# Spectral filter and sine MLP on one core: first MLP chunk of 384 tokens, sign of the imaginary filter set in the head's copy, batch 0's last stage in groups of five

## The chip, the core and the metric

The kernel runs on one core of a Trainium2 chip. The metric is the device time of one execution in microseconds (us). Three runs of the kernel before took 786.11, 786.23 and 787.95 us; the median is 786.23 us.

The engines are named as in the profile: PE is the matrix engine (PEld its weight loads), DVE the vector engine, ACT the scalar engine, POOL the GpSimd engine, and SP the engine that issues most DMAs. PSUM is the memory that PE writes to and DVE and ACT read from; SBUF is the main on-chip memory.

## The reference

```python
X = np.fft.rfft(x, axis=1)                      # x: 8 batches x 3008 positions x 256 channels
y = np.fft.irfft(X * (filt_r + 1j * filt_i), n=3008, axis=1)
x = y.reshape(8 * 3008, 256)
h = x @ w_in                                    # 256 -> 2048
g = h + np.sin(alpha * h) ** 2 / (alpha + 1e-9)
out = g @ w_out                                 # 2048 -> 256
```

Each batch goes through a Fourier filter along its 3008 positions, and each position (a token) then goes through an MLP with 2048 hidden units.

## The kernel before

**The spectral part.** 3008 is 94 times 32, so a transform of a batch is done in four matrix stages, which the profile shows by the names of their PSUM tiles: `pa` (first, line 181, 16 matmuls a batch), `pb` (forward, line 201, 12 pairs), a product with the filter on DVE (lines 215, 221 and 222), `pc` (inverse, line 232, 12 pairs) and `pd` (last, line 254, 16 groups of 4). Between the stages the data go through DRAM (`d1`, `d2`) to change their layout. The last stage writes `y`, which holds two batches side by side as columns: 94 columns for each of 32 positions `n2` of one batch. The complex product needs the real and imaginary halves of `xf` swapped; two DMAs on SP do that (`xs`, lines 208 and 209), and `cross` (lines 221 and 222) multiplies the swapped half with `f_t[1]` and adds. For that, the first 64 rows of `f_t[1]` must hold the negated imaginary filter.

**Batch 0** is done in the head, before the MLP can start, with other code: lines 396 to 507. There the imaginary part is taken by a second table `e1_0`, made by `inverse_table` (lines 364 to 372: PE transposes, then one ACT copy per group, times the per-row scale `sign`, 0.125 in the upper 64 rows and -0.125 in the lower). `other_half` copies the filter to the other 64 rows on DVE. After `turn_back`, two DVE transposes, `last_0(n0, n)` makes `y` for `n` positions `n2` from `n0` on: twice `n` matmuls (line 343) and two copies from PSUM (`evac`), the first on ACT, the second on DVE.

**The MLP** runs over chunks of tokens, 12 for each pair of batches: 11 of 512 and one of 384, the sixth. For each of the 16 hidden blocks `jb` of a chunk, `hidden` does two matmuls into PSUM (`ph`, line 541), a sine on ACT (`cos_all`, line 545, four buffers) and a DVE operation (line 546) that reads both and writes `v`. `project` multiplies a token block of 128 by `w2` in two halves of 8 matmuls (`po`, line 558); ACT copies it (line 566), and SP stores it.

**Order.** The program is written out by hand, with no scheduler: every engine takes its instructions in program order. The main loop (line 648) has 8 steps for each chunk. In a step, chunk `k` gets two hidden blocks, and the chunk before gets its share of the half projections (8 for 512 tokens, 6 for 384). Chunk 0 has no projections beside it (steps 0 to 7). All spectral work of later batches is put at a step number with `put(at, fn, ...)`, and `slot` runs what is due, twice in a step. `last_0(..., spread=True)` lays its matmuls one by one between those of the MLP (`one_between`).

**Buffers.** `fps` (2 PSUM buffers) serves `pa`, `pb`, `pc` and `pd`, `hps` (4) serves `ph`, `ops` (2) serves `po`. `vp` has two buffers. They are taken in turn by `t1_0`, `t2_0`, `w_out32` (line 473, the 32-bit output weights), and then by `v` of chunk 0, 1, 2 and so on (line 538). So `v` of chunk 1 takes the buffer of `w_out32`, and its first write waits for the last reader of that.

**Weights.** POOL scales them: `weights_in` (line 482, six pieces of `w_in` times alpha) and `weights_out` (line 514, three pieces of `w_out32`; ACT does four single blocks at steps 5 to 6.5, line 512). The four loads of `x` for batch 1 (line 141) stand between these on POOL's queue, and the first of them waits for the first half of `w_out32` to land.

**The negation.** The lower copy of the imaginary filter is made unsigned in the head, since batch 0 takes its sign from `e1_0`. Two DVE operations (`negate`, line 603) put at steps 13 and 14 negate it in place for the later batches.

`evac` without an engine named goes to ACT twice and to DVE once, in turn; every call moves the turn on.

Of the kernel before, what the change touches and what calls it, by code (L numbers as in the profile page):

```python
# [10 lines left out]
FP32 = mybir.dt.float32  # L11
# [3 lines left out]
ALU = mybir.AluOpType  # L15
# [3 lines left out]
B, S, C = 8, 3008, 256  # L19
# [43 lines left out]
def kernel(  # L63
# [10 lines left out]
    nc = tc.nc  # L74
# [17 lines left out]
    def pool(name, bufs, space=None):  # L92
        kw = {} if space is None else {"space": space}
        return ctx.enter_context(tc.tile_pool(name=name, bufs=bufs, **kw))

    cpool = pool("consts", 1)
# [10 lines left out]
    hps = pool("hps", 4, PSUM)  # L107
# [7 lines left out]
    def by_half(t):  # L115

        return t.rearrange("p a (b c) -> p (a b) c", c=128)
# [16 lines left out]
    f_t = [filt_t[:, k] for k in range(2)]  # L134
# [22 lines left out]
    def evac(dst, src, on_act=None):  # L157
        flip[0] = (flip[0] + 1) % 3
        if flip[0] if on_act is None else on_act:
            marks["act"] = nc.scalar.copy(out=dst, in_=src)  # L160
        else:
            marks["dve"] = nc.vector.tensor_copy(out=dst, in_=src)  # L162
# [108 lines left out]
    e1_0 = by_half(t4_h[1])  # L271
# [24 lines left out]
    for g in range(2):  # L296
        gs = slice(12 * g, 12 * g + 12)
        for k, filt in enumerate((filt_r, filt_i)):
            for q in range(2):
                if (g, k, q) == (0, 1, 1):  # L300
# [3 lines left out]
                    out=f_t[k][64 * k + 32 * q:64 * k + 32 * q + 32, gs, :],  # L304
# [28 lines left out]
    def last_0(n0, n, own=fps, tag="f", spread=False):  # L333

        for cb in range(2):
            made = []

            def one(i, cb=cb, made=made):

                if i == 0:  # L340
                    ps = own.tile([128, 512], FP32, name=f"pd_0_{n0}_{cb}", tag=tag)
                    made.append(ps[:, 0:n * NR].rearrange("p (a r) -> p a r", r=NR))
                nc.tensor.matmul(out=made[0][:, i, :], lhsT=t4_cols[:, n0 + i, :, cb], rhs=wi0_t,  # L343
                                 start=True, stop=True)
                if i == n - 1:
                    evac(y[:, cb, 0, n0:n0 + n, :], made[0], cb == 0)

            for i in range(n):
                if spread:
                    between.append(lambda i=i, one=one: one(i))  # L350
                else:
                    one(i)
# [4 lines left out]
        nc.tensor.transpose(out=ps[:, 0:16], in_=rec, identity=id32)  # L357
        nc.vector.tensor_scalar(out=rec_t, in0=ps[:, 0:16], scalar1=-0.5, scalar2=None, op0=ALU.mult)

    sign = cpool.tile([128, 1], FP32)  # L360
    nc.vector.memset(sign[0:64], 0.125)
    nc.vector.memset(sign[64:128], -0.125)

    def inverse_table(g):

        gs = slice(8 * g, 8 * g + 8)
        ps = ops.tile([128, 8, 128], FP16, name=f"pse_{g}", tag="o")
        for i in range(8):
            for a in range(2):
                nc.tensor.transpose(out=ps[64 * a:64 * a + 64, i, :],  # L370
                                    in_=d_t[:, 8 * g + i, 64 - 64 * a:128 - 64 * a], identity=id16)
        nc.scalar.mul(e1_0[:, gs, :], ps, sign)

    warmed = []

    def warm_pe(n):

        warmed.append(n)
        ps = hps.tile([128, 512], FP32, name=f"warm_{len(warmed)}", tag="h")
        for i in range(n):  # L380
            nc.tensor.matmul(out=ps, lhsT=idle[:, 0:128], rhs=idle[:, 0:512], start=True, stop=True)  # L381

    def other_half(g, k, on_act):

        gs = slice(12 * g, 12 * g + 12)
        evac(f_t[k][64 - 64 * k:128 - 64 * k, gs, :], f_t[k][64 * k:64 * k + 64, gs, :], on_act)

    warm_pe(10)
    def cast_x0(h):
# [6 lines left out]
    for i in range(16):  # L396
        own, tag = (fps, "f") if i % 3 == 2 else (hps, "h")
        ps = own.tile([128, 512], FP32, name=f"pa_0_{i}", tag=tag)
# [21 lines left out]
    for i in range(4):  # L420
        turn(t2_0[i // 2][:, :, 32 * (i % 2):32 * (i % 2) + 32], t1_0[:, :, 32 * i:32 * i + 32])
        if i > 1:
            other_half(0, i - 2, False)
# [56 lines left out]
    def weights_in(g):  # L480
# [4 lines left out]
        if g == 0:  # L485
            after(ins, marks["products"])

    [inverse_table(g) for g in range(2)]
    for i in range(6):
        forward_0(i)  # L490
        if i % 3 == 2:
            if i == 2: inverse_table(2)
            warm_pe((4, 0)[i // 3])
    for i in range(13):
        for e in {5: [(1,0,False)],6: [(1,1,False)]}.get(i, ()):
            other_half(*e)
        if i < 12:
            product_0(i)
        if i == 11:
            reciprocals()  # L500
        if i > 0:
            inverse_0(i - 1)
        if i + 6 < 12:
            forward_0(i + 6)
        if i == 12:
            turn_back(0)
# [12 lines left out]
    for step in ([(weights_in, g) for g in range(3)] + [(s1.load_x, 0), (weights_in, 3), (s1.load_x, 1),  # L519
# [1 line left out]
                 + [(weights_out, jb) for jb in (0, 4, 8)]):  # L521
        step[0](*step[1:])
    warm_pe(12)
    last_0(0, 4)
    last_0(4, 2, hps, "h")
    warm_pe(2)

    chunks = [(pb, c0, 384 if c0 == 2560 else 512) for pb in range(B // 2)
              for c0 in [*range(0, 2561, 512), *range(2944, 2 * S, 512)]]

    v = {}
    pso = {}
# [61 lines left out]
    def put(at, fn, *args, pe=False):  # L594
        pending.append((at, len(pending), pe, fn, args))
# [1 line left out]
    for jb in range(12, 16):  # L597
        put(5 + 0.5 * (jb - 12), weights_out, jb, 1)

    def negate(i):  # L600

        gs = slice(12 * i, 12 * i + 12)
        nc.vector.tensor_scalar(out=f_t[1][0:64, gs, :], in0=f_t[1][0:64, gs, :],
                                scalar1=-1.0, scalar2=None, op0=ALU.mult)

    for i in range(2):
        put(13 + i, negate, i)
    for n0, n, at in ((6, 5, 1.5), (11, 4, 12.5), (15, 4, 14), (19, 4, 15.5), (23, 4, 17), (27, 5, 19)):
        put(at, last_0, n0, n, fps, "f", True)
    for b in range(1, B):  # L610
        s = s1 if b == 1 else Spectral(b)
        z = 48 * b
        if b > 1:
            for ch in range(4):
                put((22,27,32,37)[ch] if b == 2 else z - 92 + 7 * ch, s.load_x, ch)
        for i in range(16):
            put(6.9 + 0.35 * i if b == 1 else 36 + 0.66 * i if b == 2 else z - 67 + 0.66 * i, s.first, i, pe=True)
        for g in range(4):
            put(12.5 if b == 1 else max(z - 56, 46.5), s.load_t2, g)
        for u in range(12):  # L620
            inv = 23.5 + 1.25 * u if b == 1 else 59 + 2.1 * u if b == 2 else z - 40.8 + 2.3 * u
            fwd = inv - (6 if b == 1 else 6)
            put(fwd, s.forward, u, pe=True)
            put(fwd + (0.5 if b == 1 else 1.5), s.product, u)
            if s.fused:
                put(fwd + (4 if b == 1 else 4.5), s.cross, u)
            put(inv, s.inverse, u, pe=True)
        for ch in range(4):
            put(z - (9.5 if b == 1 and ch < 3 else (10.5, 10.5, 10.5, 3)[ch]), s.load_t4, ch)
        for u in range(16):  # L630
            put(z + (u - (5 if b == 1 else 6.5) if u < 4 else 2 * u - 9), s.last, u, pe=True)
# [59 lines left out]
```

## Time and profile before

| what | value |
|---|---|
| median of three runs | 786.23 us (786.11 to 787.95) |
| the profiled execution | 785.94 us |
| its span, first to last instruction | 784.2 us |
| PE busy | 772.0 us (98%), 5799 matmuls |
| DVE, ACT, POOL busy | 656.1 us (84%), 617.8 us (79%), 80.0 us (10%) |
| first matmul of chunk 0 (line 541) | 36.23 us |
| first matmul of chunks 1, 2, 3, 4, 5, 6 | 46.28, 65.18, 83.04, 99.77, 117.51, 133.49 us |
| granted PE clock | 1.0 throughout |

The trace holds one execution. A time such as 46.28 counts from the start of its span. A wait is put down to the engine and line that released it last. Matmuls are pipelined: one is shown as busy until its result stands, though the next starts earlier, so the work of PE is better read from the distance between two starts than from its busy share. On DVE and ACT, too, the next instruction starts up to 0.1 us before the end of the last.

### The profile page before, as it was taken

Reading aid. Unit: us, or ns where it says so; the run is one execution under the profiler, and the core shown is the slowest. Engines: PE = TensorE matmul, PEld = TensorE weight load, DVE = VectorE, ACT = ScalarE, POOL = GpSimd, SP = SyncE. Lnnn points to the kernel's source line nnn. Section 1 sums busy time; section 2 is a strip of 40 time slices with the busy share of each in tenths; the row PEclk is TensorE's granted clock in tenths of the full one; section 3 lists DMA queues with packets and bytes.
Section 4 is the critical chain, followed back from the end, with each engine's and each line's share of the span. In section 5 each row is a group of like instructions: output and inputs, shape, how many; then the busy total and the mean of one; then the engine's idle time right before and its main releaser. Section 6 shows DMA issues by size and latency. Waiting matters only on the chain.

```text
span 784.2 us, 16619 instructions
## 1 busy us (share of the span) xinstructions
PE 772.0 (98%) x5799; PEld 535.1 (68%) x5799; DVE 656.1 (84%) x1169; ACT 617.8 (79%) x1211; POOL 80.0 (10%) x125
## 2 busy tenths in 40 slices
PE   8999999999999999999999999999999999999998
PEld 4757766676667766777667766767667776766666
DVE  7897987899878997799877998799977999777773
ACT  5897988888878887888877887788887887777674
POOL 6342000300020000200020000200002000000000
PEclk9999999999999999999999999999999999999999
DMA  9956667655664546654575454845566243421111
GB/s 218 276 118 159 130 133 221 152 124 121 172 165 89 132 101 190 148 122 107 132 206 111 104 112 132 224 90 117 121 163 174 64 99 81 116 62 28 41 41 54
DMA packets 87692, 100.99 MB, mean 129 GB/s; under 512 B 14488, under 2 KB 75944, under 8 KB 87608
## 3 DMA queue, kind: packets, MB, share of 16 engines
q1 hardware_dynamic: 78032, 73.73, 34.6%
q0 software_dynamic: 9360, 26.15, 17.9%
q8 instruction: 45, 0.74, 0.4%
q14 instruction: 39, 0.32, 0.1%
q10 hardware_dynamic: 216, 0.05, 0.0%
HBM read 55.72 MB, written 46.66 MB: 131 GB/s over the span
## 4 chain that ended last, share of the span: by engine, by line
PE 90%; DMA 4%; DVE 3%; ACT 1%; SPq 1%; issue 1%; POOL 0%; DVEq 0%; ACTq 0%; POOLq 0%
PE po L558 40%; PE ph L541 39%; PE pa L181 3%; PE pd L254 2%; PE pb L201 2%; PE pc L232 2%; DVE v L546 2%; DMA d_t<-d_tbl 1%; DMA filt_t<-in_filt_i_dram 1%; SPq L586 1%; ACT cos_all L545 1%; DMA t_a<-d 0%; PE warm L381 0%; PE pc L453 0%; DMA out_dram<-o 0%
## 5 line engine op out<-in xcount | busy, mean ns | idle before, releaser
L546 DVE SCALAR_TENSOR_TENSOR v<-cos_all,ph 128x512 f16<-128x512 f32 (+1 forms) x768 | 483.2, 672 | 106.4 <-ACT cos_all L545 102.7
L545 ACT ACTIVATE cos_all<-ph 128x512 f32<-128x512 f32 (+1 forms) x768 | 411.1, 591 | 94.4 <-PE ph L541 93.5
L558 PE MATMUL po<-w,v 128*128 128x256 f16 x3008 | 389.5, 273 | 0.0
L541 PE MATMUL ph<-y,w 128*128 128x512 f16 (+1 forms) x1536 | 387.9, 375 | 1.6 <-DVE y L162 0.9
L558 PEld LDWEIGHTS <-v 128*128 128x128 f16 x3008 | 288.2, 98 | 78.4 <-issue 2.1
L541 PEld LDWEIGHTS <-w 128*128 128x128 f16 x1536 | 147.8, 98 | 103.9 <-issue 3.1
L566 ACT COPY o<-po 128x512 f32<-128x512 f32 (+1 forms) x97 | 55.7, 574 | 19.9 <-PE po L558 12.9
L204 ACT CAST xf<-pb 128x512 f16<-128x512 f32 x84 | 50.0, 595 | 13.1 <-PE pb L201 12.3
L193 POOL DMA_DIRECT2D t<-d x56 | 36.4, 670 | 203.2 <-DMA out_dram<-o 121.6
L160 ACT CAST t_h<-pa 96x512 f16<-96x512 f32 x74 | 43.3, 585 | 8.8 <-PE pa L181 8.5
L141 POOL DMA_DIRECT2D x<-in_x_dram x32 | 17.2, 537 | 297.5 <-PE pc L232 160.4
L160 ACT CAST y<-pd 128x376 f16<-128x376 f32 (+1 forms) x82 | 39.4, 480 | 8.8 <-PE pd L254 5.3
L254 PEld LDWEIGHTS <-t_a 96*128 96x128 f16 x448 | 31.3, 97 | 19.0 <-DMA t_a<-d 0.6
L160 ACT CAST g<-pc 128x512 f16<-128x512 f32 x61 | 36.2, 593 | 9.6 <-PE pc L232 9.2
L181 PE MATMUL pa<-x,wf_t 94*96 94x512 f16 x112 | 42.4, 381 | 0.6 <-ACT t_h L160 0.4
L222 DVE TENSOR_TENSOR p<-p,xs 128x512 f16<-128x512 f16 x84 | 35.7, 425 | 2.9
L254 PE MATMUL pd<-wi_t,t_a 96*128 96x94 f16 x448 | 37.2, 204 | 0.3 <-DMA t_a<-d 0.3
L221 DVE TENSOR_TENSOR xs<-xs,filt_t 128x512 f16<-128x512 f16 x84 | 35.2, 419 | 1.5 <-DMA xs<-xf 1.5
L215 DVE TENSOR_TENSOR p<-xf,filt_t 128x512 f16<-128x512 f16 x84 | 35.2, 419 | 0.0
L232 PE MATMUL pc<-p,e_t 128*128 128x256 f16 x168 | 32.1, 273 | 1.3 <-DVE t_h L162 1.3
L201 PE MATMUL pb<-t,d_t 128*128 128x256 f16 x168 | 32.1, 273 | 0.2
L162 DVE CAST y<-pd 128x376 f16<-128x376 f32 (+2 forms) x46 | 24.9, 543 | 1.8 <-PE pd L343 1.0
(66 smaller groups left out, 264.0 us busy)
## 6 DMA issues: line engine op xcount, KB each, us to landing
x<-in_x_dram POOLq DMA_DIRECT2D x30, 376.0 KB, 5.0
d<-t_h SPq DMA_DIRECT2D x28, 384.0 KB
t<-d POOLq DMA_DIRECT2D x56, 192.0 KB, 5.0
xs<-xf SPq DMA_DIRECT2D x168, 64.0 KB
d<-g SPq DMA_DIRECT2D x56, 192.0 KB
t_a<-d SPq DMA_DIRECT2D x28, 384.0 KB
out_dram<-o SPq DMA_DIRECT2D x104, 80.0 KB
w_out<-in_moe_w_out_dram SPq DMA_DIRECT2D x2, 1024.0 KB
```

The source lines that it names most:

```text
L160: marks["act"] = nc.scalar.copy(out=dst, in_=src)
L181: marks["pe"] = nc.tensor.matmul(out=ps[0:NK, :], lhsT=wf_t, rhs=self.x[ch][:, 2 * j:2 * j + 2, :], start=True, stop=True)
L193: nc.gpsimd.dma_start(out=self.t2[g][64 * p:64 * p + 64, :, :], in_=self.d1[a0:a0 + 6, :, :].rearrange("s n c -> n s c"))
L201: nc.tensor.matmul(out=ps[:, i, :], lhsT=d_t[:, s, :], rhs=self.t2[s // 6][:, s % 6, :], start=True, stop=True)
L204: nc.scalar.copy(out=self.xf[u], in_=ps)
L232: nc.tensor.matmul(out=ps[:, i, :], lhsT=e_t[:, 2 * w + i, :], rhs=pt[:, i, :], start=(k == 0), stop=(k == len(pr) - 1))
L254: nc.tensor.matmul(out=psv[:, i, :], rhs=wi_t, start=True, stop=True, lhsT=t4_h[ch // 2][0:NK, n0 % 16 + i, cb * 128:cb * 128 + 128])
L541: nc.tensor.matmul(out=ps[:, 0:n], lhsT=w1[:, cb, jb * 128:jb * 128 + 128], rhs=y_cols[:, cb, c0:c0 + n], start=(cb == 0), stop=(cb == 1))
L545: nc.scalar.activation(out=cs[:, 0:n], in_=ps[:, 0:n], func=AFT.Sin, bias=float(np.pi / 2))
L546: marks["snake"] = nc.vector.scalar_tensor_tensor(out=v[k][:, jb, 0:n], in0=cs[:, 0:n], scalar=-1.0, in1=ps[:, 0:n], op0=ALU.add, op1=ALU. ...
L558: nc.tensor.matmul(out=pso[k][:, t % 2, :], lhsT=v[k][:, jb, 128 * t:128 * t + 128], rhs=w2[:, jb, :], start=(jb == 0), stop=(jb == 15))
L566: nc.scalar.copy(out=o[:, i0:t % 2 + 1, :], in_=pso[k][:, i0:t % 2 + 1, :])
```

## The change

Three things are changed. First, the chunk of 384 tokens in the first pair of batches is the first and not the sixth; the other three pairs keep theirs. Chunk 0 then needs 5 positions `n2` (470 columns) instead of 6 before it can start, and the head makes these in one group of 5; the later groups become (5, 5), (10, 5), and then (15, 4) and on as before. Second, `other_half` for the imaginary filter multiplies by -1 while it copies. The sign of `e1_0` is then the same in all rows, so `sign` with its two memsets goes and the ACT copy takes the constant -0.125; the two `negate` operations go. Third, for batch 1 the first stage, and the forward and inverse stages, are put at other steps.

```diff
-    sign = cpool.tile([128, 1], FP32)
-    nc.vector.memset(sign[0:64], 0.125)
-    nc.vector.memset(sign[64:128], -0.125)
...
-        nc.scalar.mul(e1_0[:, gs, :], ps, sign)
+        nc.scalar.mul(e1_0[:, gs, :], ps, -0.125)
...
-        evac(f_t[k][64 - 64 * k:128 - 64 * k, gs, :], f_t[k][64 * k:64 * k + 64, gs, :], on_act)
+        if k == 0:
+            evac(f_t[0][64:128, gs, :], f_t[0][0:64, gs, :], on_act)
+        else:
+            nc.vector.tensor_scalar(out=f_t[1][0:64, gs, :], in0=f_t[1][64:128, gs, :],
+                                    scalar1=-1.0, scalar2=None, op0=ALU.mult)
...
-    last_0(0, 4)
-    last_0(4, 2, hps, "h")
+    last_0(0, 5)
     warm_pe(2)
 
-    chunks = [(pb, c0, 384 if c0 == 2560 else 512) for pb in range(B // 2)
-              for c0 in [*range(0, 2561, 512), *range(2944, 2 * S, 512)]]
+    chunks = [(pb, c0, 384 if c0 == 0 else 512) for pb in range(B // 2)
+              for c0 in [0, *range(384, 2 * S, 512)]]
+    chunks[12:] = [(pb, c0, 384 if c0 == 2560 else 512) for pb in range(1, B // 2)
+                   for c0 in [*range(0, 2561, 512), *range(2944, 2 * S, 512)]]
...
-    def negate(i):
-
-        gs = slice(12 * i, 12 * i + 12)
-        nc.vector.tensor_scalar(out=f_t[1][0:64, gs, :], in0=f_t[1][0:64, gs, :],
-                                scalar1=-1.0, scalar2=None, op0=ALU.mult)
-
-    for i in range(2):
-        put(13 + i, negate, i)
-    for n0, n, at in ((6, 5, 1.5), (11, 4, 12.5), (15, 4, 14), (19, 4, 15.5), (23, 4, 17), (27, 5, 19)):
+    for n0, n, at in ((5, 5, 1.5), (10, 5, 12.5), (15, 4, 14), (19, 4, 15.5), (23, 4, 17), (27, 5, 19)):
         put(at, last_0, n0, n, fps, "f", True)
...
-            put(6.9 + 0.35 * i if b == 1 else 36 + 0.66 * i if b == 2 else z - 67 + 0.66 * i, s.first, i, pe=True)
+            put(7.7 + 0.31 * i if b == 1 else 36 + 0.66 * i if b == 2 else z - 67 + 0.66 * i, s.first, i, pe=True)
...
-            inv = 23.5 + 1.25 * u if b == 1 else 59 + 2.1 * u if b == 2 else z - 40.8 + 2.3 * u
+            inv = 24.2 + 1.23 * u if b == 1 else 59 + 2.1 * u if b == 2 else z - 40.8 + 2.3 * u
```

The forward stage of a unit stays 6 steps ahead of its inverse stage, and `cross` 4 steps after the forward stage, so both move with `inv`.

## The prediction

> **What bounds the kernel now.** First the page: busy shares and clock.
>
> ```profile
> PE 772.0 (98%) x5799; PEld 535.1 (68%) x5799; DVE 656.1 (84%) x1169; ACT 617.8 (79%) x1211; POOL 80.0 (10%) x125
> ...
> PEclk9999999999999999999999999999999999999999
> ```
>
> PE is the bound and its clock is whole. The change leaves the number and kinds of matmuls as they are, so only the start of chunk 0 and PE's waits can move the end. I read the waits from the distance between matmul starts: undisturbed, a `ph` matmul takes 0.216 us at 512 tokens and 0.162 at 384, a `po` 0.109, a `pa` 0.22, a `pd` 0.04. What exceeds that from 36.2 us on is 11.0 us: 2.3 in chunk 0 (36.2 to 46), 0.7 to 58, 1.6 to 66, 0.6 to 76, 0.1 to 110, 1.4 at 112.9, 0.8 from 120 to 140, and 3.4 spread over the other 640 us. So anything to be won lies before 130 us. Next, who ended PE's waits there (waits of PE, 36 to 200 us: total, times, longest):
>
> ```profile
> PE pc L232 <- DVE t_h L162: 1.3, 1, 1.3
> PE ph L541 <- DVE y L162: 0.9, 1, 0.9
> PE ph L541 <- DVE v L546: 0.6, 1, 0.6
> ...
> PE pd L254 <- DMA t_a<-d: 0.3, 1, 0.3
> ```
>
> These few waits are what the change can touch. Then DVE in time order, 36 to 50 us (start, length, operation):
>
> ```profile
> 37.55 4.87 DVE L546 SCALAR_TENSOR_TENSOR v<-cos_all,ph 128x512 f16<-128x512 f32 x8 [1.10 <-ACT cos_all L545]
> 42.34 0.64 DVE L162 CAST y<-pd 128x470 f16<-128x470 f32 x1
> 42.89 3.67 DVE L546 SCALAR_TENSOR_TENSOR v<-cos_all,ph 128x512 f16<-128x512 f32 x6
> 46.78 1.29 DVE L546 SCALAR_TENSOR_TENSOR v<-cos_all,ph 128x512 f16<-128x512 f32 x2 [0.22 <-ACT cos_all L545]
> 47.98 0.68 DVE L162 CAST t_h<-pa 96x512 f16<-96x512 f32 x1
> 48.90 1.28 DVE L546 SCALAR_TENSOR_TENSOR v<-cos_all,ph 128x512 f16<-128x512 f32 x2 [0.24 <-POOL w L514]
> ```
>
> Chunk 0 is bound by DVE, 0.60 us a block; PE would need 0.43. The last row carries the forecast: the first `v` of chunk 1 starts 0.03 us after POOL's last `w2` piece. It takes the buffer of `w_out32`. POOL's own rows:
>
> ```profile
> 36.19 0.58 POOL L141 DMA_DIRECT2D x<-in_x_dram  x1 [1.48 <-PE pd L343]
> ...
> 43.27 5.59 POOL L514 TENSOR_TENSOR w<-w_out,rec_t 128x1024 f16<-128x1024 f32 x3
> ```
>
> From 36.19 to 48.87 POOL has no gap, and nothing in that queue is changed. DVE in 60 to 68 us:
>
> ```profile
> 60.82 0.95 DVE L603 TENSOR_SCALAR filt_t<-filt_t 64x3072 f16<-64x3072 f16 x1
> ...
> 63.38 0.95 DVE L603 TENSOR_SCALAR filt_t<-filt_t 64x3072 f16<-64x3072 f16 x1
> 64.25 0.54 DVE L162 CAST y<-pd 128x376 f16<-128x376 f32 x1
> ```
>
> The second negation stands ahead of the `y` copies, the last of which (65.90 to 66.44) releases chunk 2's second matmul at 66.49.
>
> The Trainium skill ("Perfetto Trace Analysis", section Identifying the Most-Contended Engine) says that matmul busy share is no measure of headroom, since matmuls are pipelined. By the share, 784.2 - 772.0 = 12.2 us is idle; by the starts, 19.0 us over the span is lost, so the rule holds here.
>
> **The change, part by part.**
>
> *Head.* The negating copy takes 0.947 us (row of line 603, same shape) for 0.955 of the plain copy: nothing. The two `sign` memsets (0.06 us each, at 3.14) stand before a DVE wait for `x` until 5.05: nothing. The ACT copy with a constant isn't in the trace; by its own row, 1.11 us, it costs the same. It ends at 20.1, while the head waits for the filter's DMA until 24.25, so up to 1 us either way is hidden. Ten `pd` matmuls instead of twelve save 0.19 us on PE. But the second `ph` matmul waits for DVE's copy of `y`: the last `pd` starts at about 35.53, DVE follows 0.30 later (35.34 to 35.64 now) and takes 0.64 for 470 columns: 36.47, now 36.45. A shorter 384-token matmul lets the first `v` start at about 37.43 instead of 37.55. Bounds for the head: -0.3 to +0.2; I take the first `ph` at 36.05 for 36.23.
>
> *Chunk 0.* A `v` of 384 takes a DVE turn of 0.47 us, a sine an ACT turn of 0.38 (384-token rows of chunk 5). DVE: 37.43 + 16 x 0.47 + 0.56 for one copy = 45.5; ACT with four weight blocks of 0.40 puts the last `v` at about 46.2, for 48.06 now. PE's work falls from 6.9 to 5.2 us; these 1.7 us come back in chunk 5. So the wait ratio stays; only about 0.3 us is won here.
>
> *The new wait.* DVE's next operation is `v` of chunk 1, and that waits for POOL until 48.87: DVE stands still for 2.7 us, where it now loses 0.24. Behind it in DVE's queue are three more `v` and the copy of `pa_2`. PE goes on with what it may: `ph_0` to `ph_3` of chunk 1 fill the four `hps` buffers (to 46.65), `pa_2` waits for ACT's copy of `pa_0` (47.0), eight `po` (0.88) and `pa_3` follow, and at 48.3 `ph_4` needs the first `v`, which ends at 48.90 + 0.68 = 49.58. That is 1.3 us of PE wait, and no other work covers it. (PE to 49.62: 5.6 of chunk 0 with its `pd`, 1.7 for four `ph`, 0.9 for `po` and 0.9 for `pa` are 9.1 of 13.6 us; the 4.5 of waits are 2.2 in chunk 0, 1.0 between the four `ph`, and the 1.3.)
>
> *Steps 8 to 15.* I carried PE, ACT and DVE on from 49.62 in program order by the row lengths (a reader follows a matmul's start by 0.41 us). With 6 instead of 8 half projections, steps 8 and 12 have none, and the `pa` come closer (0.31 step for 0.35; three together in step 12). The two `fps` buffers then wait for their copies: `pa_5` 0.3, `pa_7` 0.5, `pa_12` 1.0, the first `pd` of group 10 0.5, small ones 0.2: 2.5 us, and chunk 2 starts at 65.0. PE's work to there: 5.2 + 6.9 + 5.2 (48 `po`) + 3.5 + 1.1 = 21.9, so waits are 65.0 - 36.05 - 21.9 = 7.05. Now, to 66.49: 6.9 + 6.9 + 7.0 + 3.5 + 1.1 + 0.2 = 25.6, waits 66.49 - 36.23 - 25.6 = 4.65. Both negations' stalls (0.5 and 1.1) are gone in the first sum. **+2.4 us of waits, -0.2 for the head: +2.2.** Bounds: the four named copy waits may all vanish (-2.3) or double (+2.3).
>
> *112.9 us.* DVE sits behind `cross` of unit 11, whose swap DMAs are issued at 107.16 to 108.71, behind seven stores (3.35 us) on SP, and land at 110.2; DVE loses 1.55, PE 1.4. In the new order six stores stand there (-0.48), and two more `v` (1.2 us) stand before that `cross` on DVE: 1.68 of relief against 1.55. I take -1.2, bounds -1.4 and +0.5. The `pd` wait at 125.2 (0.5, for the load of `t_a`) has the same distance on PE (11.3 us of work for 11.4): 0, bounds -0.5 and +0.5.
>
> *The rest.* Evacuations change engines by the shifted turn, in stages where PE waits 3.4 us in 640: 0, bounds -0.3 and +0.3. SP gets one store DMA more, 752 for 751, among stores that PE doesn't wait for.
>
> Sum: 785.94 + 2.2 - 1.2 = **786.9 us**, against the profiled execution; that one stands 0.3 below the median of 786.23. So +0.1%, no change: 0.3%, 2.4 us, is about what a measurement of this kernel tells from none.
>
> The Trainium skill ("SBUF — State Buffer", section Who interferes with whom) says that a VectorE operation with one SBUF input and outside the two-port modes does not hold up GpSimd. `v` has one (its other input is `ph`), and POOL's product of 768 took 1.82 us beside transposes, 1.83 beside `v`. By the rule, idle DVE doesn't hasten POOL and the sum stays.
>
> **The rivals.**
>
> 1. *The swap stall stays* (+1.4 for -1.2 and a bit): 785.94 + 2.2 = 788.1. For it: SP issues 10 us without a gap before it now. Against: the two `v`.
>
> 2. *Slower: the two `fps` buffers pace steps 8 to 15.* Place: `pa_4` to `pa_15`. A buffer's turn is matmul 0.41, copy 0.59 to 0.68, and up to two queued sines or `v` (0.98 to 1.2). If every pair pays it, the stage's copy waits are 4.6, not 2.3. It decides once these waits pass 4.1 us in sum. Price: +2.3: 786.9 + 2.3 = 789.2. For it: ACT and DVE are at 17.2 and 18.1 busy of 20.6 us there. Against: the negations' 1.9 us of DVE are gone.
>
> 3. *Faster: the buffer hand-over costs PE nothing.* If the wait for POOL falls away (1.3) and with it the copy waits behind it (2.3), it is 786.9 - 3.6 = 783.3: the shorter chunk, the missing negations and the swap relief all count. For it: PE's wait there is only 1.3 long and later ones could absorb it. Against: the row at 48.90.
>
> 4. *The negation was not what held chunk 2.* Then its 1.1 us would return as another wait for `y`: 788.0. Against: group (10, 5) alone covers chunk 2 (1410 columns, 1408 needed), and it is ready three steps early.
>
> **How the numbers follow.** Forecast 0.50; rival 1 0.15; rival 2 0.15; rival 3 0.12; rival 4 0.05; 0.03 left for more than rival 2. The forecast's own bounds (785.5 to 788.2) hold rivals 1 and 4. To leave no more than 2 in 10 outside, the range reaches to rival 2's time and two thirds of the way to rival 3's: 784.4 to 789.2. Faster by over 0.3% (below 783.9): rival 3, 0.12. Slower (above 788.6): rival 2 and the rest, 0.18. Within: 0.70.
>
> **What would show it.** The first `v` of chunk 1 at 48.9 with DVE idle 2 to 3 us before it, released by POOL; a PE wait of about 1.3 us before 49.6; `pa` waits on ACT and DVE copies until 62 us; chunk 2 at about 65; no DVE wait for `xs` near 111. The forecast is wrong if POOL ends well before 48.9, if chunk 2 starts before 63.5 or after 67, or if a wait over 1 us appears after 130 us.

## The result, and the profile after

The changed kernel takes **790.4 us** (median of six runs, 788.9 to 791.94) where the kernel before takes 786.39 (six runs, 786.11 to 787.95): a ratio of 1.0048, 95% interval 1.0037 to 1.0059. It is slower by 4.0 us, 3.5 us above the forecast of 786.9 and outside the range. The profiled execution took 791.03 us with a span of 789.2.

The page of the changed kernel, busy times and PE's clock:

```profile
PE 771.8 (98%) x5799; PEld 534.5 (68%) x5799; DVE 654.0 (83%) x1164; ACT 617.4 (78%) x1210; POOL 79.4 (10%) x125
...
PEclk9999999999999999999999999999999999999999
```

PE's work and clock are as before; the 5.0 us that the span has grown are waits. Who ended PE's waits from 36 to 130 us (total, times, longest):

```profile
PE ph L542 <- DVE v L547: 2.1, 4, 1.5
PE pb L201 <- ACT xf L204: 1.6, 1, 1.6
PE ph L542 <- POOL w L482: 1.3, 2, 0.7
PE pa L181 <- ACT t_h L160: 1.0, 2, 0.8
PE pc L232 <- ACT g L160: 0.7, 1, 0.7
PE pb L201 <- DMA t<-d: 0.7, 1, 0.7
```

Of before's waits, the 1.3 us of `pc`, the 0.9 for `y` and the 0.3 for `t_a` are gone, the 0.6 of `ph` for `v` has grown to 2.1 and the 0.4 of `pa` for ACT's copy to 1.0; the waits of `pb`, the one of `pc` for ACT and that for `w_in` pieces are new. DVE in order of time around the hand-over of the buffer (start, length, operation, idle time before it):

```profile
46.28 1.02 DVE L547 SCALAR_TENSOR_TENSOR v<-cos_all,ph 128x384 f16<-128x384 f32 x2 [0.53 <-ACT cos_all L546]
50.36 2.48 DVE L547 SCALAR_TENSOR_TENSOR v<-cos_all,ph 128x512 f16<-128x512 f32 x4 [3.06 <-POOL w L514]
52.76 0.68 DVE L162 CAST t_h<-pa 96x512 f16<-96x512 f32 x1
```

DVE stands still for 3.06 us, until 0.03 us after POOL's last `w2` piece. POOL's rows:

```profile
30.21 4.84 POOL L482 TENSOR_TENSOR w<-w_in,y 128x768 f16<-128x768 f32 x3 [13.08 <-DVE rec_t L358]
37.62 0.58 POOL L141 DMA_DIRECT2D x<-in_x_dram  x1 [2.57 <-PE ph L542]
...
44.73 5.59 POOL L514 TENSOR_TENSOR w<-w_out,rec_t 128x1024 f16<-128x1024 f32 x3
```

POOL is idle from 35.05 to 37.62. The row names PE, but the instruction waits for the first half of `w_out32`, whose landing is seen only as a semaphore at 37.08. In before the same wait lasted 1.48 us.

The excess of PE's start distances over undisturbed ones, by stretch, worked out as in the prediction. A second trace of the changed kernel (e13 below) stands beside the first:

| stretch, us | before | changed, first | changed, second |
|---|---|---|---|
| 0 to 36.2 | 8.0 | 8.1 | 8.1 |
| 36.2 to 44 | 2.0 | 3.0 | 2.3 |
| 44 to 50 | 0.9 | 2.7 | 2.3 |
| 50 to 58 | 0.2 | 1.9 | 1.9 |
| 58 to 66 | 1.6 | 0.7 | 0.7 |
| 66 to 78 | 0.6 | 1.5 | 1.2 |
| 94 to 120 | 1.5 | 2.7 | 2.8 |
| 120 to 140 | 0.8 | 0.1 | 0.1 |
| the rest | 3.5 | 3.3 | 3.3 |
| sum | 19.0 | 24.0 | 22.7 |

The sums differ as the spans do: 784.2, 789.2 and 787.9 us.

### The profile page after: what moved, and what is told of

Same layout as the page of the kernel before. It is cut to its first block, busy times and chain, and to the rows that moved or that the text cites. A ratio compares the mean times of both kernels' runs of the same rounds, so it can differ in the third digit from the quotient of the medians.

```text
span 789.2 us, 16619 instructions
## 1 busy us (share of the span) xinstructions
PE 771.8 (98%) x5799; PEld 534.5 (68%) x5799; DVE 654.0 (83%) x1164; ACT 617.4 (78%) x1210; POOL 79.4 (10%) x125
## 4 chain that ended last, share of the span: by engine, by line
PE 87%; DMA 5%; POOL 2%; ACT 2%; issue 2%; DVE 1%; SPq 1%; POOLq 0%; ACTq 0%
PE po L559 39%; PE ph L542 38%; PE pa L181 3%; PE pd L254 2%; PE pb L201 2%; PE pc L232 2%; DMA e_t<-e_tbl 1%; DMA w_out<-in_moe_w_out_dram 1%; DMA d<-g 1%; SPq L587 1%; POOL w L514 1%; DVE v L547 1%; DMA xs<-xf 1%; POOL x L141 0%; DMA t<-d 0%
## 5 line engine op out<-in xcount | busy, mean ns | idle before, releaser
L162 DVE CAST t_h<-pa 96x512 f16<-96x512 f32 x38 | 25.8, 680 | 0.4 <-PE pa L181 0.4
```

## The experiments

Ratios are to runs of the kernel before on the same chip, whose medians lay between 786.57 and 786.73 us; intervals are 95%.

**Which part: e1, e2, e13.** e1 is before with the sign hunks of the diff alone. e2 is the changed kernel with

```diff
-            put(7.7 + 0.31 * i if b == 1 else ...
+            put(6.9 + 0.35 * i if b == 1 else ...
-            inv = 24.2 + 1.23 * u if b == 1 else ...
+            inv = 23.5 + 1.25 * u if b == 1 else ...
```

and e13 is the changed kernel, unedited.

> The kernel before with the sign part alone: negating copy in the head, constant -0.125, no negations at steps 13 and 14; chunks, groups and put steps as before. Theory (the negations held chunk 2, the changed kernel's loss comes from POOL and the put steps): the stalls of 0.5 and 1.1 us near 62 and 66 us go, so about 784.8 us against 786.4. Rival (the negations only stood beside another wait for y): 786.4 again. Second rival (the sign part itself costs something in the head or later): 787.5 or more.

> The changed kernel with the put steps of before (6.9 + 0.35 i, 23.5 + 1.25 u). Theory (the new put steps cost about 2 us: PE waits of 0.85 and 0.6 near 73 to 77 us for the t2 loads and 1.77 and 0.88 near 104 to 106 us for the swap, less the 1.4 and 0.5 that before lost at 112.9 and 125.2): about 788.3 us. Rival (all of the loss is in chunks 0 and 1, from POOL and the two fps buffers, and the DMA waits only move again): 790.4. The waits on POOL before 51.1 us must stand in both cases.

> The changed kernel once more, for a second trace of it. Theory: PE's waits on POOL in chunk 0 (1.3 us), on v of chunk 1 (1.5 us), and near 104 to 106 us (2.6 us) come from the order and stand again; about 790.4 us. Rival (they came from the late filter DMA of that one execution: L475 was reached at 27.7 us for 26.5): with an early filter DMA POOL's chain ends near 48.9 us and these waits shrink by 1.4 us, 789 us.

e1: 786.51 us, 0.9996 (0.9987 to 1.0006). The sign part is worth nothing. PE's waits in e1:

```profile
PE ph L541 <- DVE y L162: 0.8, 1, 0.8
```

Before `ph` of chunk 2 there is still a wait for `y` (0.9 in before), though no negation stands in DVE's queue. My theory fell; the first rival was right. (e1 also moves the turn of the copies by two, since the copy of the imaginary half no longer goes through `evac`, so it tests the two together.)

e2: 793.7 us, 1.0086 (1.0070 to 1.0102), so the old steps cost 3.3 us more, not 2 less. PE's waits:

```profile
PE pa L181 <- ACT t_h L160: 2.4, 4, 0.8
PE pb L201 <- DMA t<-d: 2.3, 1, 2.3
PE pa L181 <- DVE t_h L162: 2.0, 1, 2.0
```

With the shorter first chunk, earlier `pa` run into DVE while it waits for POOL, and an earlier `pb` into its load. Behind the longest of these waits, which ends at 51.70 us, PE's granted clock falls to 0.50 (53 to 55 us), and eight `po` take 1.91 us, where eight just before the wait take 1.04:

```profile
53.09 1.91 PE L559 MATMUL po<-w,v 128*128 128x256 f16 x8
```

The clock is at half for 3.4 us, an estimated 1.7 us of lost work. Five of e2's six runs have a mean clock of 0.995 to 0.998; the one at 1.0 took 791.14 us. So a good part of the 3.3 us goes with the clock. At the swap the old steps lose less, as the theory had it: the excess from 94 to 120 us is 1.2 in e2.

e13: 790.18 us, 1.0037 (1.0024 to 1.0050). In this execution the filter's DMA released SP's first `w_in` load at 22.40 us, for 23.29 in the first trace (22.21 in before). POOL is 1.06 us earlier, and PE has no wait for a `w_in` piece:

```profile
PE ph L542 <- DVE v L547: 2.3, 4, 1.4
PE pb L201 <- ACT xf L204: 1.7, 1, 1.7
PE pa L181 <- ACT t_h L160: 1.0, 2, 0.8
PE pc L232 <- ACT g L160: 0.7, 1, 0.7
```

So the 1.3 us on `L482` change with the execution (the traces of e2 and e18, with POOL's order unchanged, have 0.3 and 0.5), and the other waits belong to the kernel: the theory holds for these, the rival for that one. The second trace is the better witness against before.

**The waits on POOL: e3, e4, e8.** e3 is the changed kernel with

```diff
-    [(weights_in, g) for g in range(3)] + [(s1.load_x, 0), (weights_in, 3), (s1.load_x, 1),
-                 (weights_in, 4), (s1.load_x, 2), (weights_in, 5), (s1.load_x, 3)]
+    [(weights_in, g) for g in range(4)] + [(s1.load_x, 0), (weights_in, 4), (s1.load_x, 1),
+                 (weights_in, 5), (s1.load_x, 2), (s1.load_x, 3)]
```

In e4, besides, the third `w_out` piece goes from POOL to DVE:

```diff
-                 + [(weights_out, jb) for jb in (0, 4, 8)]):
+                 + [(weights_out, jb) for jb in (0, 4)]):
...
+    put(7.2, weights_out_dve, 8, 4)    # the same product with nc.vector
```

e8 is before with the sign part and e3's order.

> The changed kernel with the fourth piece of w_in ahead of the first load of x on POOL's queue, so that POOL works while the first half of w_out lands; nothing else moves. POOL's last piece of w_out should end near 48.3 us for 50.33. Theory (PE's 1.26 us of waits for w_in pieces and 1.69 us for v of chunk 1 come from POOL's 2 us of idle time): these waits fall to 0.3 or less together, about 787.7 us. Rival (the copies from the two fps buffers set the pace of steps 8 to 15): PE arrives earlier and waits at pa and pd instead, 789.5 or more.

> As the third run, and the last of POOL's three w_out pieces is done by DVE at the end of chunk 0 instead, in DVE's idle time. POOL should be done near 46.4 us and DVE's idle 3 us before v of chunk 1 should be gone, for about 1.1 us of DVE work. Theory (the buffer shared by w_out and v of chunk 1): both waits gone, about 787.4 us, no worse than the third run. Rival (fps copies set the pace): no gain over the third run or a loss, since DVE has more to do, 789.5 or more.

> The kernel before with the sign part, and with the POOL order of the third run. Theory (with a first chunk of 512 POOL's chain ends together with DVE's work for chunk 0, so that it costs at most the 0.24 us of DVE's idle time): 786.0 to 786.5 us, no difference that can be told. Rival (POOL's idle time costs the kernel before as well, through the w_in pieces and v of chunk 1): 785 us or less.

e3: 789.27 us, 1.0024 (1.0006 to 1.0042). POOL's last piece ends at 47.9 us:

```profile
42.30 5.59 POOL L514 TENSOR_TENSOR w<-w_out,rec_t 128x1024 f16<-128x1024 f32 x3
```

The excess from 44 to 50 us falls from 2.3 (second trace) to 0.8, and the time by about 1 us by the medians. The wait is real, and it is only about a quarter of the loss; the time lies nearer to the rival's 789.5 than to the theory's 787.7. e4: 789.07 us, 1.0030 (1.0019 to 1.0041): DVE's own work takes the place of the wait, and PE's excess from 50 to 58 us rises from 1.7 to 2.4. e8: 786.29 us, 0.9990 (0.9975 to 1.0004): in the kernel before this wait costs nothing that can be told.

**The two `fps` buffers and the t2 loads: e6, e7.** Both start from e3:

```diff
+            own, tag = (hps, "h") if self.b == 1 and i % 3 == 2 else (fps, "f")    # e6, in first()
-            inv = 24.2 + 1.23 * u if b == 1 else ...
+            inv = 25.0 + 1.18 * u if b == 1 else ...                               # e7
```

> The third run, and every third pa tile of batch 1 comes from hps (as batch 0's do) instead of fps. Theory (PE's waits at pa of 0.27, 0.49 and 0.99 us in steps 8 to 15 are waits for the turn of the two fps buffers): they fall to 0.5 or less together, chunk 2 starts some 1.2 us earlier, near 62.8 us for 64.04, about 788.0 us at most, if the earlier start isn't lost to the t2 loads. Rival (ACT and DVE are full there and set the pace, whichever buffer is used): the waits move to ph and chunk 2 starts at 64 us again, 789.3.

> The third run, and batch 1's forward and inverse stages start 0.8 step later at a slightly closer distance (25.0 + 1.18 u for 24.2 + 1.23 u). Theory (pb near 70.6 us waits for the t2 loads; the swap wait near 101 us comes from which DMA stands eight issues ahead on SP's queue and so moves with the put steps): the wait at the first pb is gone (0.6 us), the swap stall is elsewhere or gone: 786 to 789 us. Rival (the forward stage's distance to the DMAs isn't what matters): the same waits at the same units, 789.3 us.

e6: 788.87 us, 1.0025 (1.0010 to 1.0040). Its lines are one higher:

```profile
PE pa L182 <- DVE v L548: 1.3, 1, 1.3
PE pb L202 <- DMA t<-d: 1.3, 1, 1.3
PE pb L202 <- ACT xf L205: 1.2, 1, 1.2
```

No `pa` waits for a copy any more, and chunk 2 starts at 62.96 us, as expected. So the four copy waits (2.3 us) were the two buffers' turn. But `pa_2` now waits 1.3 us for a `ph` buffer behind a `v`, and `pb`, reached earlier, waits 1.3 for its load where e3 waits 0.4. Of the 1.1 us won at chunk 2, 0.2 are left at chunk 3 (81.15 for 81.38). e7: 788.52 us, 1.0017 (1.0003 to 1.0030). The wait for the load is gone, and the swap's stall is still there, at 96.8 (1.1) and 103.5 us (1.2). The theory holds for the load; the swap's stall has moved by a unit and not shrunk.

**The swap: e5, e9, e10, e18, e15.** e5, e9 and e10 start from e3; e18 is the changed kernel with e10's edit alone; e15 is e8 with it.

```diff
-                    nc.sync.dma_start(out=self.d2[a0:a0 + 6, ...   # e5: nc.scalar, e9: nc.gpsimd, for b == 1
...
-                put(fwd + (4 if b == 1 else 4.5), s.cross, u)
+                put(fwd + (3 if b == 1 else 4.5), s.cross, u)      # e10, e15, e18
```

> The third run (fourth piece of w_in ahead on POOL), and batch 1's stores of g to d2 are issued on ACT's queue instead of SP's. Theory (SP's queue stands still for a store of g that takes 6 us to land, so the swap DMAs of xf are issued late; that is PE's 1.65 and 0.88 us of waits near 101 to 104 us): these waits fall below 0.5 us together, 789.3 - 2.2 = about 787.1 us. Rival (the swap is late through SP's own issue rate or the landing, whoever stores g): waits of 2 us or more stay in 95 to 115 us, 789 us or more, the issues costing ACT a little.

> The third run (fourth piece of w_in ahead on POOL), and batch 1's stores of g are issued by POOL, whose DMAs use other semaphores than those of SP and ACT. Theory (a swap DMA is issued late because SP's DMA waits for the DMA eight issues earlier on the same semaphore, which is a 6 us store of g, and because SP has no gap there; on ACT the store kept the same eight semaphores): PE's waits of 1.65 and 0.88 us near 101 to 104 us fall below 0.6 us together, 789.3 - 2 = about 787.2 us. Rival (the ring of three xs buffers sets the swap's pace: the swap of unit u waits for the cross of unit u - 3): the stall stays at 2 us or more, 789 us.

> The third run, and batch 1's cross is put 3 steps after its forward stage instead of 4, so that its xs buffer comes free before the swap of three units later is issued. Theory of the ring (SP stands up to 2 us for a cross with swaps, stores of g and output stores behind it): SP's waits for DVE fall away, PE's 2.5 us near 101 to 104 us fall below 0.8, about 787.3 us. Rival (semaphore of a store of g, or SP's issue rate): DVE now waits for xs earlier instead, and the same or more is lost, 789 us or more.

> The changed kernel with cross 3 steps after forward instead of 4 and nothing else; POOL's order as in the changed kernel. Theory (the ring's stall is apart from the waits on POOL): 2.1 to 2.7 us less than the changed kernel, 787.7 to 788.3 us. Rival (the tenth run's gain needed POOL's earlier end, as all stages then lie 2 us earlier): 789.5 us or more.

> The kernel before with the sign part, the POOL order of the third run and cross 3 steps after forward instead of 4. Theory (before's stall of 1.4 us at 112.9 us is the same ring of three xs buffers behind SP's queue): the stalls from 105 to 115 us fall below 0.4 us, 785.0 to 785.8 us. Rival (the ring matters only with the changed kernel's steps): 786.3 us, as the eighth run.

e5: 790.2 us, 1.0039 (1.0025 to 1.0053): three waits of 0.85, 0.88 and 1.03 us for the two. Issued by ACT, the stores of `g` keep the semaphores that SP's DMAs wait on; my theory of what the move would free fell. e9: 788.43 us, 1.0026 (1.0018 to 1.0035): `pb`'s 1.5 is gone, `pc`'s 0.9 stays, and `pd` waits 1.3 for `t_a`, whose load follows those stores. So the stretch from 94 to 120 us falls from 2.5 (e3) to 1.0, and from 120 to 140 us 1.5 come back. e10: **787.17 us**, 1.0010 (1.0001 to 1.0019), 2.1 us below e3 by the medians and 1.1 by the ratios; e18: 789.16 us, 1.0029 (1.0019 to 1.0039), 1.0 to 1.2 us below the changed kernel's two medians, though the intervals overlap. SP's own waits from 70 to 112 us, first in the second trace of the changed kernel and then in e18:

```profile
SPq L208 <- DVE p L222: 2.0, 1, 2.0
SPq L208 <- DMA xs<-xf: 1.7, 1, 1.7
...
SPq L208 <- DMA d<-g: 0.6, 1, 0.6
```

```profile
SPq L208 <- DMA out_dram<-o: 0.9, 1, 0.9
SPq L208 <- DVE p L222: 0.6, 1, 0.6
```

There are three `xs` buffers, so SP must wait with the swap of unit u for the `cross` of unit u - 3, and everything behind it in SP's queue waits too. SP also waits for earlier DMAs to land, of `xs`, `g` and the output. From the end of the `xf` copy to the end of the issue of its swap, us:

| unit | 4 | 5 | 6 | 7 | 8 | 9 | 10 | 11 |
|---|---|---|---|---|---|---|---|---|
| before | 3.8 | 3.4 | 2.3 | 3.2 | 4.0 | 4.8 | 5.2 | 7.9 |
| changed, second trace | 6.0 | 4.1 | 2.5 | 7.2 | 7.9 | 6.0 | 3.1 | 4.8 |
| e18 | 4.1 | 2.2 | 1.4 | 5.0 | 5.1 | 4.0 | 3.6 | 5.0 |
| e10 | 3.8 | 1.9 | 1.1 | 4.9 | 4.3 | 2.6 | 3.0 | 4.4 |
| e9 | 4.7 | 2.8 | 2.5 | 5.6 | 4.9 | 4.4 | 1.7 | 3.1 |

With three `xf` buffers as well, ACT can't copy unit 10 before the swap of unit 7 has landed: its row in the first trace

```profile
103.67 0.58 ACT L204 CAST xf<-pb 128x512 f16<-128x512 f32 x1 [3.27 <-DMA xs<-xf]
```

is what holds `pb`, and the sines queued behind it. In e18 neither `pb` nor `pc` waits for ACT, yet the excess from 94 to 120 us falls only from 2.8 to 1.7: what is left, little more than before's 1.5, are waits of 0.3 us and less, spread over the stretch. The ring is shown to be a cause, though the time came out between the two expectations. It is not shown to be the only one: e9 leaves the ring as it is, takes the stores of `g` out of SP's queue, and lowers the delay of unit 7 and this stretch about as much as e10 does (to 1.0 in both). How the stall divides between the ring and the stores, these runs don't tell. e15: 786.7 us, 0.9994 (0.9985 to 1.0003): nothing for the kernel before. The delay of unit 11 is 4.8 us, for 7.9 in before and 5.4 in e8, but the earlier `cross` comes to meet it, and DVE waits 1.38 us for the swap at 108.9; the rival was right there. In this stretch there was little left to win: e8, from which e15 starts, has 0.5 us of excess there, and e15 1.6.

**Do the waits add up: e11, e14, e12.** e11 joins e3, e6, e7 and e9; e14 joins e3, e6 and e10 with `inv = 24.7 + 1.23 * u`; e12 is before with the sign part, e3, e9 and

```diff
-    ... (11, 4, 12.5), ...
+    ... (11, 4, 11.5), ...
```

> The changed kernel with four mends at once: fourth piece of w_in ahead on POOL, every third pa from hps, forward and inverse 0.8 step later at 1.18, stores of g of batch 1 issued by POOL. Theory (the loss is a sum of separate waits, each with its own release): excess of PE's start distances 21.2 in the third run less about 1.7 at pa and pd, 1.2 at pb and pd near 70 us, 2 for the swap, and 1 to 1.4 more at pa_2 = about 17.5 us, so 785.3 us. Rival (the waits stand in for one another, since ACT, DVE and SP are nearly full up to 110 us): 787.5 us or more, with the waits at other places.

> The changed kernel with POOL's fourth piece of w_in ahead, every third pa of batch 1 from hps, cross 3 steps after forward instead of 4, and the forward and inverse stages half a step later at the old distance (24.7 + 1.23 u). Theory (separate waits, which add up when the ring of xs buffers is not tightened): from the tenth run's excess of 20.3 us, less 2.3 at pa and pd, plus 1.4 at pa_2, less 1.1 near 70 to 75 us = 18.3, about 785.2 us. Rival (ACT and DVE are full and the waits only change places): 787.2 us, as the tenth run, or more.

> The kernel before with the sign part, the POOL order of the third run, the stores of g of batch 1 issued by POOL, and the group of four positions from 11 on put one step earlier (11.5). Theory: chunk 2's second matmul no longer waits 1 us for the copy of y, and the swap stall near 112 us is gone: 786.3 - 1.0 - 0.5 = about 784.8 us. Rival (the wait for y moves to another copy, and POOL's DMAs are slower): 786.3 us or more.

e11: 787.66 us, 1.0014 (1.0005 to 1.0023). e14: 787.9 us, 1.0016 (1.0003 to 1.0028), no better than e10, which has fewer mends. Its waits:

```profile
PE ph L543 <- DVE v L548: 2.6, 5, 1.5
PE pa L182 <- DVE v L548: 1.3, 1, 1.3
PE pb L202 <- ACT cos_all L547: 0.7, 1, 0.7
PE pd L255 <- DMA t_a<-d: 0.6, 1, 0.6
```

The rivals were right in both: up to 125 us the waits largely stand in for one another. e12: 789.42 us, 1.0033 (1.0020 to 1.0046), my poorest guess: the wait for `y` fell to 0.2, but there are 1.1 us at `pa`, 1.1 at `pb`, and, as in e9, 1.5 for `t_a`. No version here beats the kernel before by more than its interval.

**Groups or turn of the copies: e16, e17.** e16 is the changed kernel with before's groups; e17 adds the line of `flip` to it.

```diff
-    last_0(0, 5)
+    last_0(0, 4)
+    last_0(4, 2, hps, "h")
+    flip[0] = (flip[0] + 1) % 3    # e17 alone
     warm_pe(2)
...
-    for n0, n, at in ((5, 5, 1.5), (10, 5, 12.5), (15, 4, 14), ...
+    for n0, n, at in ((6, 5, 1.5), (11, 4, 12.5), (15, 4, 14), ...
```

> The changed kernel with batch 0's last stage in the groups of before: four and two in the head, then (6, 5) and (11, 4) at the same steps; the chunk of 384 stays first, the sign part and the put steps stay. Theory (the grouping is worth only two pd matmuls and one wait in the head): 790.4 to 791.0 us. Rival (the group of five in the head or (10, 5), with one position more at step 12.5, costs copy waits): 789.5 us or less.

> The sixteenth run (groups of before in the changed kernel) with the turn of the copies moved on by one after the head, so that the copies of pa_0 and pa_1 are ACT's again and not one of them DVE's. Theory (the sixteenth run's 2.1 us at the fourth pa is a copy that stood on DVE behind the v that waits for POOL): that wait is gone, 795.1 - 2.1 = 793 us at most, and 790.4 to 791.0 if the 2.4 us of its late head do not return. Rival (the groups themselves, or a head made slower by them, cost the 5 us): 794 us or more.

e16: 795.14 us, 1.0101 (1.0084 to 1.0117), outside both expectations. PE in order of time:

```profile
49.65 1.04 PE L560 MATMUL po<-w,v 128*128 128x256 f16 x8
52.74 0.38 PE L181 MATMUL pa<-x,wf_t 94*96 94x512 f16 x1 [2.05 <-DVE t_h L162]
```

The four copies of the head's groups, for two, move the turn: an early `pa` is now copied by DVE, behind the `v` that waits for POOL. e17: 790.14 us, 1.0046 (1.0032 to 1.0059). With the turn set back the 2.05 us are gone and the time is the changed kernel's: the grouping is worth nothing, and with the turn go 5.0 us. Of the 6.1 us between the two spans about 1.9 are a late head (first `ph` at 38.62 for 36.76 in e17, see the last section) and 2.05 the wait. Behind the wait PE's granted clock is at half again for 3.4 us (0.59 from 53 to 55 us, 0.56 from 55 to 57), an estimated 1.7 us:

```profile
54.69 1.91 PE L560 MATMUL po<-w,v 128*128 128x256 f16 x8
```

So the copy on the wrong engine cost nearly twice its wait.

## Why the prediction was wrong, point by point

*Head.* First `ph` 36.05 forecast; 36.35 and 36.13 measured. Right, within what the executions differ: 35.72 to 36.93 in the thirteen traces with this head, so that the 0.1 us is partly luck. The filter's DMA, later in the first trace, may be the reason for the spread; that wasn't tested.

*Chunk 0.* Last `v` forecast at 46.2; it starts at 45.8 and ends at 46.4 in the second trace. Right. The first trace has 1.3 us for `w_in` pieces that I didn't think of, since POOL was taken to be where it was in before.

*The new wait.* Forecast: DVE idle 2.7, PE 1.3, POOL done at 48.87. Measured in the second trace: 2.95, 1.6 and 49.27. Right, and e3 shows that POOL is its cause.

*Steps 8 to 15.* Four waits of 0.3, 0.5, 1.0 and 0.5 us were named; 0.27, 0.50, 0.99 and 0.53 came, at the matmuls named, and e6 shows that the buffers make them. Chunk 2 starts at 65.42 in the second trace (65.0 forecast). For the stretches up to 66 us the forecast sum was +2.2; measured, +2.6. One reason in it was wrong: the negations didn't hold chunk 2 (e1, rival 4's reading). The wait for `y` fell because the third chunk now ends at token 1408 and needs 15 positions instead of 17; it stays away in e17 with before's groups.

***112.9 us: the step that failed.*** The prediction took -1.2 us here, because "two more `v` (1.2 us) stand before that `cross` on DVE: 1.68 of relief against 1.55". Measured from 94 to 120 us: 2.8 for 1.5, so **+1.3**. These 2.5 us are most of the miss. The relief itself came: the 1.4 us that `pc` lost at 112.9 are gone. What the prediction put at nothing is a new stall eight to ten microseconds earlier, 1.8 us at `pb` and 0.9 at `pc` (to 103.0 and 105.0 in the second trace). I had looked at one unit, the last, and at the stores just ahead of its swap. The swaps are a chain through SP, the `cross` and three buffers, and it is the late swap of unit 7 (issued 7.2 us after its `xf`) that stops ACT at unit 10, which takes the same buffer. e10 and e18 show it: `cross` one step earlier takes 1.1 to 2.1 and about 1.1 us off. The stores of `g` in SP's queue (e9) and the new put steps (e2) have a part in it, whose size stays open.

*Terms that were priced at nothing.* 66 to 78 us: +0.6 (`pb` waits 0.55 for the t2 loads and a `pd` 0.6 for a buffer that ACT's copy of `xf` holds, where before loses 0.5 in all; in e7, with the forward stage later, these waits are gone). `t_a` at 125.2: -0.7. Sum against before, second trace: 2.6 + 0.6 + 1.3 - 0.7 and -0.1 in the rest is 3.7 us, which is the difference of the spans. The one store DMA more on SP (752 for 751), which was priced at nothing, isn't in the traces: SP issues 888 DMAs in both, 595 of them of the output.

*The rivals.* The first (the swap stall stays) was right that the swap costs PE, but not in the place: the stall that it named went, and the new one was not in its price. The second (the buffers pace steps 8 to 15) came near in time, by another road: those waits were 2.3, not 4.6. The third fell with POOL's row.

What stays open: in e14 `ph` waits 1.7 us for `v` at 108.8 us, where the swap's stall was mended; whether a better order would remove it wasn't settled. That chunk 0 with 384 tokens must cost something wasn't shown either, only that none of these mends won it back.

## What to carry to other kernels

A stall at the end of a chain of transfers is not priced at its last link: list, unit by unit, the delay between producer and transfer, and see which buffer count closes the ring. Where several waits are short and the engines around them nearly full, take each mend for an upper bound; the three of e14 (with the forward stage put later besides), worth about 1, 0.4 and 2 us by the medians one by one, gave no more together than two of them. A copy's place in an in-order queue can matter more than its length: where engines take turns, follow the turn past every wait that the change brings. And a wait of PE can cost more than its length, when the clock falls behind it, as in e2 and e16.

## What the runs showed of the hardware

In the first trace a store of `g` took 6.44 us from issue (93.73) to landing (100.17), and the swap DMA eight issues later on SP, which counts on the same one of eight semaphores, waited for that. The Trainium skill ("Perfetto Trace Analysis", section DMA Instruction — HWDGE (DVE, Sync)) says that a DMA's row ends when its issuing is done, and that the semaphore may follow surprisingly late when the target is HBM. This trace agrees: the row of that store is 0.62 us long.

In e16 PE waited 0.97 and 0.76 us for `x` between 5 and 9 us, and its granted clock then fell. The columns are the stretch, its length, five engines' busy time, PE's clock, DMA share and GB/s:

```profile
5.00:8.00 3.00, 2.03 (x8) 0.60 (x7) 2.18 (x3) 0.58 (x1) 1.22 (x3) 1.00 1.07 216
8.00:10.00 2.00, 1.24 (x5) 0.53 (x4) 1.44 (x3) 0.39 (x2) 0.85 (x3) 0.75 1.06 209
10.00:12.00 2.00, 2.00 (x6) 0.63 (x5) 0.87 (x2) 0.91 (x2) 1.71 (x6) 0.50 1.13 306
```

Its head ended about 2 us late. The Trainium skill ("TensorE: Matmul & The Clock Gate", section Part 1: The HAM clock gate (the "warmup" mystery)) has PE fall back to half clock after an idle window of about 3.4 us. Here shorter ones were enough: two waits of 1.7 us in sum, with matmuls between them, and later one of 2.05 us; in e2 one of 1.98. In the second trace of the changed kernel a wait of 1.66 us left the clock at 1.0. Where the line lies wasn't tested. All four runs of e16 had a mean clock of 0.996 to 0.998 and all five of e17, with the same head, 1.000. The means don't tell where the clock fell in the three runs that have no trace, so how much of e16's 5 us is the head's stays open.
